# VectorE's exp groups as whole key rows, with the PV banks from the common pool

## The chip, the cores and the metric

The kernel runs on one core of one Trainium2 chip. The metric is the device time of one execution in microseconds (us). Each figure is the median of several runs; the 95% intervals come from rounds in which a kernel and the kernel before ran on the same chip.

Names: PE is TensorE, PEld its weight loads, DVE VectorE, ACT ScalarE, POOL GpSimd. A "bank" is one of the eight PSUM banks.

## The reference, cut to what matters

```python
x = A_x                                     # [1, 2048, 512], bf16
h  = x + attention(layernorm(x)) @ wo       # 32 heads of 16, softmax over 2048 keys
h2 = h + (gelu(layernorm(h) @ w_gate) * (layernorm(h) @ w_up)) @ w_down   # F = 1792
```

Attention over 32 heads of 2,048 x 2,048 scores dominates: 2,048 score tiles of 128 keys by 512 queries. The exponentials are the largest work.

## The kernel before

The kernel is a Python scheduler. It holds streams of operations with planned durations, lets the best-ranked operation that is ready go next, and so fixes one order of instructions for each engine. On the chip the engines follow these orders and wait for each other by semaphores.

A unit is one head group and query chunk: 16 key rows of four tiles. The four tiles of a row (index `g`) belong to four heads; their score matmuls use four row tiles of the PE array (32 rows each), their products with V four column tiles. ScalarE takes tiles in pairs, in order, through two pairs of banks. VectorE takes some tiles out of order, in groups of four: a conversion from PSUM (`dXE<-pbank`), two bit operations and one product (a "chain") make two fp16 factors, which cost PE two products with V per tile.

A VectorE score matmul should ride along: issued right behind a ScalarE pair, on a row tile that the pair leaves idle, it costs nearly nothing. So the scheduler plans it as `TDQ = 0.02` us. `sch.wake` holds the row tiles that the last pair used.

```python
def pick(G):                              # kernel before: the tile for a VectorE group
    ...
    cand = [i for i in range(i0, min(unit0[u + 1], i0 + AWIN))
            if i not in own and TILES[i][2] not in G["g"] | sch.wake]   # scattered over 4 rows
    return cand[0] if cand else None

def dget():
    ...
                b = yield Acquire(gate=...)           # a bank
                i = pick(G)                           # the tile is chosen here ...
                own[i] = ("d", G["k"])
                fns, rd = scores([(i, b)])
                wk = sch.wake | {TILES[i][2]}
                yield Op("pe", TDQ if TILES[i][2] not in sch.wake else TST, mode="r", ...)  # ... issued later
                sch.wake = wk
                sch.add(dconv(G, len(G["t"]), b), -2)
```

The products with V gather in a bank of their own, and a finished unit is copied out, transposed in a bank from the common pool, and scaled.

```python
PVB = 4                 # the bank for products with V
DENSE = (5, 6, 7)       # the pool for everything else
...
def ofin(u):
    yield Op("dve", 0.6, tensor_copy(OA, pbank[:, PVB, :]))
    b = yield Acquire(...)                         # a pool bank
    yield Op("pe", 4 * TTR, four transposes of OA into bank b)
    yield Op("dve", 0.165, reciprocal(...))        # reads bank b
    ... yield Op("dve", ..., tensor_tensor(Otok, ...))   # reads bank b
    sch.release(b)
...
sch.add(ofin(u), -1.0)                             # lower numbers go first
```

## Time and profile before

| kernel before | |
|---|---|
| time | 845.3 us (844.34 to 845.38) |
| span in the profile | 843.2 us |
| exps of ScalarE | 796 pairs = 1,592 tiles |
| tiles of VectorE | 456 |
| last exp ends / rest after it | 807.4 / 35.8 us |
| excess of exp intervals over 0.9035 us (those under 2 us) | 32.0 us |
| score steps / products with V of ScalarE's tiles (PE, sums of start to start) | 299 / 134 us |

How to read it: the exp records overlap, so the idle time before them understates ScalarE's lateness. The last two rows are counted from the trace's starts instead, for PE from the weight loads, of which the trace has all. The page's lines for this kernel are in the prediction below.

One more view of the kernel before, the waits: who waited for whom, us in all, times, longest.

```profile
PEld pbank L1272 <- ACT PT L1278: 221.0, 546, 1.0
PEld pbank L1272 <- DVE dXE L1590: 18.3, 50, 0.5
DVE dXE L1590 <- PE pbank L1272: 12.8, 35, 1.0
```

The first is idle time of the weight loader until ScalarE had freed a score pair's banks. It is not PE's idle time: in 215 of the 221 us matmuls issued earlier were still running, fillers among them (matmuls on zeros, `ones_bf,zero_bf`, that the scheduler puts into planned gaps of PE). So it is used only as a sign of which engine came last, not as an amount of time to be won. The other two are the exchange of pool banks for VectorE's tiles.

### The profile page before, as it was taken

Reading aid. Unit: us, or ns where it says so; the run is one execution under the profiler, and the core shown is the slowest. Engines: PE = TensorE matmul, PEld = TensorE weight load, DVE = VectorE, ACT = ScalarE, POOL = GpSimd, SP = SyncE. Lnnn points to the kernel's source line nnn. Section 1 sums busy time; section 2 is a strip of 40 time slices with the busy share of each in tenths; the row PEclk is TensorE's granted clock in tenths of the full one; section 3 lists DMA queues with packets and bytes.
Section 4 is the critical chain, followed back from the end, with each engine's and each line's share of the span. In section 5 each row is a group of like instructions: output and inputs, shape, how many; then the busy total and the mean of one; then the engine's idle time right before and its main releaser. Section 6 shows DMA issues by size and latency. Waiting matters only on the chain.

```text
span 843.2 us, 16693 instructions
## 1 busy us (share of the span) xinstructions
PE 819.5 (97%) x6773; PEld 254.4 (30%) x6773; DVE 769.0 (91%) x1246; ACT 786.3 (93%) x833; POOL 42.9 (5%) x100
## 2 busy tenths in 40 slices
PE   8999999999999999999999989999999989999997
PEld 3222222222222222222222222222233333333455
DVE  7569999999999999999989989999999999899862
ACT  3979999999999999999999999999999999999941
POOL 5600000000010000000010000000010000000000
PEclk9999999999999999999999999999999999999999
DMA  6000004300000000000000000000000000000000
GB/s 200 1 1 1 1 2 160 116 1 1 8 7 1 2 1 2 7 26 7 2 14 1 1 1 2 7 26 7 2 21 7 2 1 2 2 26 14 2 13 18
DMA packets 12327, 15.06 MB, mean 18 GB/s; under 512 B 1744, under 2 KB 11216, under 8 KB 12240
## 3 DMA queue, kind: packets, MB, share of 16 engines
q1 hardware_dynamic: 12240, 13.90, 5.0%
q8 instruction: 55, 0.90, 0.4%
q14 instruction: 32, 0.26, 0.1%
HBM read 11.80 MB, written 2.10 MB: 16 GB/s over the span
## 4 chain that ended last, share of the span: by engine, by line
PE 75%; ACT 12%; DVE 6%; issue 5%; POOL 1%; ACTq 0%; POOLq 0%; DVEq 0%
PE pbank L1272 46%; PE pbank L1271 21%; ACT PT L1278 11%; PE pbank L1870 3%; DVE dXE L1590 2%; DVE dXE L1607 1%; PE pbank L1275 1%; ACT GUT L1809 1%; PE pbank L1867 1%; PE pbank L1880 1%; DVE dXE L1605 1%; POOL xn_sb L1369 1%; DVE dW L1604 1%; PE pbank L1725 0%; PE pbank L1747 0%
## 5 line engine op out<-in xcount | busy, mean ns | idle before, releaser
L1278 ACT ACTIVATE PT<-pbank 128x1024 bf16<-128x1024 f32 x796 | 742.3, 1072 | 17.7 <-PE pbank L1272 14.6
L1272 PE MATMUL pbank<-QT,KT 32*128 32x512 bf16 x2048 | 345.0, 384 | 7.2 <-ACT PT L1278 4.9
L1590 DVE TENSOR_SCALAR dXE<-pbank 128x512 uint16<-128x512 f32 x456 | 296.9, 682 | 15.9 <-PE pbank L1272 12.8
L1272 PEld LDWEIGHTS pbank<-QT,KT 32*128 32x128 bf16 x2048 | 84.2, 91 | 311.5 <-ACT PT L1278 220.8
L1272 PE MATMUL pbank<-PT,VA 128*17 128x512 bf16 (+1 forms) x1992 | 149.4, 339 | 0.1
L1607 DVE TENSOR_TENSOR dXE<-dW,dXE 128x2048 f16<-128x2048 f16 (+1 forms) x115 | 139.1, 1210 | 2.0
L1604 DVE TENSOR_SCALAR dW<-dXE 128x2048 uint16<-128x2048 uint16 (+1 forms) x115 | 78.1, 679 | 0.8
L1605 DVE TENSOR_SCALAR dXE<-dXE 128x2048 uint16<-128x2048 uint16 (+1 forms) x115 | 78.1, 679 | 0.0
L1272 PE MATMUL pbank<-dXE,VA 128*17 128x512 f16 (+1 forms) x1136 | 70.3, 339 | 0.0
L1271 PE MATMUL pbank<-hnT_c,wu_sb 128*128 128x512 bf16 (+1 forms) x280 | 59.7, 346 | 7.4 <-DVE GUT L1823 6.8
L1271 PE MATMUL pbank<-hnT_c,wg_sb 128*128 128x512 bf16 (+1 forms) x280 | 65.5, 340 | 0.0
L1271 PE MATMUL pbank<-wd_sb,GUT 128*128 128x512 bf16 x224 | 59.2, 382 | 0.0
L1272 PEld LDWEIGHTS pbank<-PT,VA 128*17 128x17 bf16 x1992 | 39.2, 88 | 65.3 <-issue 57.8
L1870 PE MATMUL pbank<-ones_bf,zero_bf 128*128 128x512 bf16 x168 | 55.7, 386 | 0.0
L1823 DVE TENSOR_TENSOR GUT<-pbank,GUT 128x512 bf16<-128x512 f32 x56 | 37.3, 685 | 16.0 <-PE pbank L1271 12.8
L1741 POOL TENSOR_SCALAR rstd<-mv 128x1 f32<-128x1 f32 x16 | 6.6, 413 | 761.0 <-DVE mv L1739 761.0
L1271 PE MATMUL pbank<-xnT,wqkv_sb 128*128 128x512 bf16 x128 | 37.8, 383 | 0.0
L1271 PEld LDWEIGHTS pbank<-hnT_c,wu_sb 128*128 128x128 bf16 x280 | 23.5, 99 | 32.5 <-issue 11.8
L1797 DVE CAST GUT<-pbank 128x512 bf16<-128x512 f32 x49 | 33.1, 680 | 0.0
L1271 PEld LDWEIGHTS pbank<-hnT_c,wg_sb 128*128 128x128 bf16 x280 | 19.5, 97 | 27.8 <-issue 20.6
L1272 PEld LDWEIGHTS pbank<-dXE,VA 128*17 128x17 bf16 x1136 | 18.7, 88 | 29.8 <-issue 24.0
L1271 PEld LDWEIGHTS pbank<-wd_sb,GUT 128*128 128x128 bf16 x224 | 17.0, 97 | 27.0 <-issue 14.3
(82 smaller groups left out, 390.8 us busy)
## 6 DMA issues: line engine op xcount, KB each, us to landing
xres<-in_A_x_dram SPq DMA_DIRECT2D x16, 128.0 KB, 2.2
out_dram<-out_sb SPq DMA_DIRECT2D x16, 128.0 KB, 1.7
wg_sb<-in_B_w_gate_dram SPq DMA_DIRECT2D x1, 1792.0 KB, 7.1
wu_sb<-in_B_w_up_dram SPq DMA_DIRECT2D x1, 1792.0 KB, 11.2
wd_sb<-in_B_w_down_dram SPq DMA_DIRECT2D x1, 1792.0 KB, 17.4
x_sb<-in_A_x_dram SPq DMA_DIRECT2D x3, 512.0 KB, 8.3
wqkv_sb<-in_A_wqkv_dram SPq DMA_DIRECT2D x1, 896.0 KB, 7.5
x_sb<-in_A_x_dram SPq DMA_DIRECT2D x2, 256.0 KB, 2.9
```

Source lines behind the costliest of these rows:

```text
L1271: return lambda e: e.matmul(o, l, r, start=start, stop=stop)
L1272: return lambda e: e.matmul(o, l, r, start=start, stop=stop, tile_position=tile)
L1275: return lambda e: e.transpose(out=o, in_=i, identity=idn)
L1278: return lambda e: e.activation(out=o, in_=i, func=func, **kw)
L1369: lambda e: e.tensor_scalar(out=xn_sb[:, t % 8, :], in0=x_sb[:, t, :], scalar1=rstd[:, tt_], scalar2=htmp[:, tt_], op0=ALU.mult, op1=ALU.add),
L1590: yield Op("dve", 0.603, lambda e: e.tensor_scalar(out=dXE[G["k"] % NX][:, 0, j, :], in0=pbank[:, b, :], scalar1=XMIN + 1024.0 * CENTER, s ...
L1604: yield Op("dve", t1, lambda e: e.tensor_scalar(out=W.bitcast(U16), in0=X, scalar1=0x3ff, scalar2=0xb800, op0=ALU.bitwise_and, op1=ALU.bit ...
L1605: yield Op("dve", t1, lambda e: e.tensor_scalar(out=E, in0=X, scalar1=0x7c00, scalar2=0x8, op0=ALU.bitwise_and, op1=ALU.bitwise_or), reads ...
L1607: yield Op("dve", t2, lambda e: e.tensor_tensor(out=X.bitcast(F16), in0=W, in1=X.bitcast(F16), op=ALU.mult), reads=kW + kX, writes=kX, por ...
L1797: yield Op("dve", 0.6, lambda e: e.tensor_copy(out=o_ap, in_=i_ap), reads=[("pb", b)], writes=keys, extra=dE)
L1823: yield Op("dve", 0.6, lambda e: e.tensor_tensor(out=o_ap, in0=u_ap, in1=o_ap, op=ALU.mult), reads=[("pb", b)] + keys, writes=keys)
L1870: fill_op = Op("pe", TMM, lambda e: e.matmul(pbank[:, PVB, :], zero_bf[:], ones_bf[:], start=False, stop=False, skip_group_check=True), re ...
```

## The change

Its intent: a VectorE group becomes one whole key row, so that what is left for ScalarE is whole rows too, and products with V always fill four column tiles. Products with V take a bank from the pool, so that a second unit can open before the first is copied out. A second buffer for the chain and fewer gates keep more groups in flight; VectorE starts after 12 projections instead of 20. `behind()` is to pace dense work. The option to give products to GpSimd is zero. The core of the diff, cut:

```diff
-PVB = 4
-DENSE = (5, 6, 7)
+DENSE = (4, 5, 6, 7)
+DMAX = 3
+KEND = 2
+PACE = 1.0
+DB = 1
+CHP = -2.1
+NPOOL = 0
-AHEAD = 12
+AHEAD = 8
-DFROM = 20
+DFROM = 12
...
+            u, i0 = find()                       # the next free whole row
+            G = C["gopen"] = dict(u=u, t=[], row=range(i0, i0 + 4), k=C["gk"], conv=0)
+            for i in G["row"]:
+                own[i] = ("d", G["k"])
...
-                b = yield Acquire(gate=lambda: "qkdone" in C or over(G) or pick(G) is not None)
+                b = yield Acquire(gate=lambda: pick(G) is not None and C["dout"] < DMAX - (DB if behind() else 0))
                 i = pick(G)
...
-        cand = [i for i in range(i0, min(unit0[u + 1], i0 + AWIN)) if i not in own and TILES[i][2] not in G["g"] | sch.wake]
+        cand = [i for i in G["row"] if i not in G["t"] and (ANYG or TILES[i][2] not in sch.wake)]
...
-            sch.add(ofin(u), -1.0)
+            sch.add(ofin(u), -1.0).dyn = lambda: -3 if C["oa"] <= u else -1.0
...
+                    pvbank[u] = yield Acquire(prio=-20, gate=lambda: u not in pvbank and u - 1 <= C["oa"])
...
+        sch.add(group_pv(G), -5.1)               # products of a VectorE group: a stream of its own
```

## The prediction

> **What bounds the kernel now.** I read the page first, for the engines' shares and the costliest groups.
>
> ```profile
> PE 819.5 (97%) x6773; PEld 254.4 (30%) x6773; DVE 769.0 (91%) x1246; ACT 786.3 (93%) x833; POOL 42.9 (5%) x100
> L1278 ACT ACTIVATE PT<-pbank 128x1024 bf16<-128x1024 f32 x796 | 742.3, 1072 | 17.7 <-PE pbank L1272 14.6
> L1272 PE MATMUL pbank<-QT,KT 32*128 32x512 bf16 x2048 | 345.0, 384 | 7.2 <-ACT PT L1278 4.9
> L1590 DVE TENSOR_SCALAR dXE<-pbank 128x512 uint16<-128x512 f32 x456 | 296.9, 682 | 15.9 <-PE pbank L1272 12.8
> L1607 DVE TENSOR_TENSOR dXE<-dW,dXE 128x2048 f16<-128x2048 f16 (+1 forms) x115 | 139.1, 1210 | 2.0
> L1870 PE MATMUL pbank<-ones_bf,zero_bf 128*128 128x512 bf16 x168 | 55.7, 386 | 0.0
> ```
>
> There are 2,048 score tiles of 128x512. ScalarE exponentiates 1,592 of them in 796 pairs; VectorE does 456 in 115 groups. All three large engines look nearly full, and ScalarE waited only 17.7 us before its exps, so one would say that ScalarE is the bound. That reading is too quick. I therefore took the starts of the 796 exps from the trace: 454 of the 795 intervals are 0.90 us, the pace of ScalarE when nothing holds it. The excess of the longer intervals over 0.9035 us, leaving out the seven of over 2 us (four of them hold a GELU), is 32 us; the longer ones without a GELU add some 5. A record is 1.02 to 1.3 us long and overlaps the next, so a wait inside an interval hardly shows as idle time. About 9 of these 32 us lie between 40 and 100 us, some 27, with the waits of over 2 us, between 100 and 800.
>
> The timeline shows who holds them. PE matmuls and exps, first where exps keep their pace, then where they do not (start, length, engine, line; xN is the number of matmuls):
>
> ```profile
> 151.83 0.39 PE L1272 MATMUL pbank<-QT,KT 32*128 32x512 bf16 x4
> 152.16 0.61 PE L1272 MATMUL pbank<-dXE,VA 128*17 128x512 f16 x8
> 152.75 0.39 PE L1272 MATMUL pbank<-QT,KT 32*128 32x512 bf16 x3
> ...
> 153.61 0.60 PE L1272 MATMUL pbank<-QT,KT 32*128 32x512 bf16 x3
> 154.14 0.61 PE L1272 MATMUL pbank<-PT,VA 128*17 128x512 bf16 x8
> 154.69 0.39 PE L1272 MATMUL pbank<-QT,KT 32*128 32x512 bf16 x2
> ```
>
> ```profile
> 754.12 0.60 PE L1272 MATMUL pbank<-QT,KT 32*128 32x512 bf16 x3
> 754.65 0.82 PE L1271 MATMUL pbank<-wd_sb,GUT 128*128 128x512 bf16 x3
> 755.40 0.39 PE L1272 MATMUL pbank<-QT,KT 32*128 32x512 bf16 x3
> 755.73 0.82 PE L1271 MATMUL pbank<-wd_sb,GUT 128*128 128x512 bf16 x3
> 756.48 0.60 PE L1272 MATMUL pbank<-QT,KT 32*128 32x512 bf16 x3
> ```
>
> PE alternates between one score pair and one slot of other work. A score step of 0.39 takes 0.32 from its start to the next start, one of 0.60 takes 0.53; a slot takes 0.54, or 0.75 with three dense matmuls. The usual turn is 0.32 + 0.54 = 0.86 us, just under ScalarE's 0.90. A doubled score step makes it 1.07, and so do three down-projection matmuls. Two pairs of score banks let PE be one step late, no more. So **PE sets the pace in part of the turns, ScalarE in the others, and VectorE is close behind**: its busy time by windows is 671 of the 700 us from 100 to 800 and 62.8 of the 80 us from 20 to 100.
>
> ```profile
> 20.00:40.00 20.00, 18.69 (x137) 5.83 (x136) 13.15 (x31) 18.69 (x20) 15.42 (x39) 1.00 0.00 1
> 40.00:100.00 60.00, 59.89 (x410) 14.87 (x408) 49.65 (x77) 54.27 (x59) 0.00 (x0) 1.00 0.00 1
> ```
>
> In these windows (PE, PEld, DVE, ACT, POOL) PE is full of projections, VectorE is partly idle, and its first exp tile comes only at 52.7 us.
>
> **What the Trainium skill says.** "TensorEngine Tiling (Array Packing)", Key Properties: tiles of the array work independently, and a change of the tiling mode drains TensorE. The trace agrees with both: two to four score matmuls on different row tiles take 0.39 us like one, and a step costs about 0.10 us over its 0.22 of streaming. "TensorE: Matmul & The Clock Gate", Back-to-back issue gap: N/2.4 + 2.5 ns warm, 216 ns for 512 columns; here a second matmul of the same tile lengthens a step by 0.21 to 0.22 us. "VectorE: DVE Perf Modes", Why PSUM operands drop a tier: fp32 from PSUM runs at the basic rate. Agrees: 0.68 us for 512 elements from PSUM, the same as for 2,048 of 16 bits in the mask operations. "Perfetto Trace Analysis", Identifying the Most-Contended Engine: matmul busy time is no good measure. It is so here: the 97% holds 203 filler matmuls (168 on L1870, 35 on L1880).
>
> **The change part by part.**
>
> Whole rows, products of the ScalarE tiles with V. Their four tiles of a key row stand on four column tiles and run together; a slot handles two rows. Today VectorE takes scattered tiles, so a slot of 5, 6 or 7 matmuls still lasts as long as one of 8: in the trace's order of matmuls 119 such slots of the 512-wide units, and of those with 4 only about 20, take the short 0.33. All 256 slots cost at most 512 steps of 0.215 us, less about 20. With whole rows the 1,592 tiles make 398 steps. Saved: (512 - 20 - 398) x 0.215 = **20 us of PE**.
>
> Whole rows, scores. With scattered tiles the next two ScalarE tiles can lie on the same row tile and run after each other. 141 score steps in the trace cost 0.5 to 0.62 instead of 0.32. With whole rows the pairs are always (0,1) or (2,3), and a VectorE tile is taken only on an idle row tile. Saved: up to 141 x 0.215 = **30 us of PE**. Together 50 us, of some 780 us of attention.
>
> Products of VectorE tiles: 115 groups with two products per tile, 0.43 us each, unchanged. They become a stream of their own, so the unit's last products no longer wait in line for a chain.
>
> VectorE: nothing is removed. A group costs 4 x 0.60 + 2 x 0.61 + 1.14 = 4.76 us start to start (timeline). "All products stay" means that GpSimd takes none. The doubled dW and the lifted gate keep two groups in flight, and the start after 12 instead of 20 projections lets VectorE use idle time before 52 us. One group more takes two ScalarE steps away, 1.81 us.
>
> PV banks: one bank joins the three common ones. While one unit is open there are three others, as now; at a unit's end two are held, leaving two. This removes the wait for the eviction of the PV bank (0.68 us, 32 times, mostly hidden), and costs some bank pressure.
>
> Pacing: chunk 4's up and down products now run at 798 to 816 us, beside the last exps (ending at 807.4). Finished earlier, they free the way to the tail's first gate product at 819.4: **1 to 2 us**. The tail itself stays.
>
> **The sum.** Of the 36 us of late exps, about 8 come from three-matmul down steps and stay; from the early projections perhaps half of 9. I take 17 us as removed. VectorE now does 734 us between 20 and 800; in a stretch 17 us shorter, at 96.5% use, 736 fit: its share stays at about 115 groups, or 2 more at 98% (3.6 us). So 17 + 1 to 3 + 1 to 2: about 20 us, 825. Bank pressure is the one cost I can't size; for it I add 2: **827 us**.
>
> **Rivals.** First, VectorE becomes the bound: with PE free it has only 29 us idle from 100 to 800, 22.7 of it before exp operations as gaps that nobody's wait explains. If it cannot fill them, it loses groups as the span shrinks, each giving 1.8 us back to ScalarE: gain 10 to 12, time 833 to 836. Second, banks: with two PV banks held and up to three VectorE tiles outstanding, dense work lacks banks, falls behind, and the pace check cuts VectorE's tiles; then 838 to 848. For it: VectorE's largest named wait is already for scores (12.8 us). Against: a unit lasts 24 us and the overlap a few. Third, the gain is larger: stalls vanish, early VectorE idle time gives three groups, the tail 3 us: 814 to 818. Fourth, ScalarE was the bound after all and freed PE time turns to fillers: 840.
>
> **Range and chances.** The 2% line is 828.4. First and main case lie on both sides of it. 8 in 10: 815 to 841. Faster 0.53, same 0.43, slower 0.04.
>
> **What would show it.** Right: nearly no score step of 0.60; slots of V products with 4 or 8 matmuls only, the 4s short; the excess of exp intervals down from 32 to under 18 us; VectorE tiles 448 to 476; VectorE at 96% or more from 100 to 800; more PE idle or fillers; a first VectorE exp before 40 us. Wrong: VectorE tiles under 440 (first rival), or waits of dense work and of L1590 for banks at unit ends (second). Few late exps but no shorter span would mean that what PE gave was taken back in VectorE's share.

## More of the kernel before

All runs used here are with a mean granted TensorE clock of 0.988 to 1.0. Where one of the smaller differences may hang on the clock, the text says so.

A planned duration that is wrong does not make the result wrong, only the order ill-chosen.

One line of the page that the prediction does not show, the products with V of ScalarE's tiles:

```profile
L1272 PE MATMUL pbank<-PT,VA 128*17 128x512 bf16 (+1 forms) x1992 | 149.4, 339 | 0.1
```

VectorE operations that read a pool bank are lifted to rank -2.2 (`HELD`), unless their stream has a rank of its own (`dyn`).

## The result, and the profile after

The changed kernel took **864.5 us** (863.73 to 865.05), against 845.3: the ratio is 1.0232, with a 95% interval of 1.0218 to 1.0247. It is slower by over 2%. Ratios are the mean time of one kernel's fast runs over that of the other's of the same rounds, so not quite the ratio of the medians.

The page of the changed kernel, for the lines shown of before:

```profile
PE 824.8 (96%) x6713; PEld 261.6 (30%) x6822; DVE 770.2 (89%) x1229; ACT 796.3 (92%) x835; POOL 41.2 (5%) x100
L1295 ACT ACTIVATE PT<-pbank 128x1024 bf16<-128x1024 f32 x800 | 754.9, 1039 | 23.7 <-PE pbank L1289 17.1
L1289 PE MATMUL pbank<-QT,KT 32*128 32x512 bf16 x2048 | 377.4, 383 | 12.4 <-ACT PT L1295 5.9
L1601 DVE TENSOR_SCALAR dXE<-pbank 128x512 uint16<-128x512 f32 x448 | 299.1, 686 | 30.9 <-PE pbank L1289 25.5
L1619 DVE TENSOR_TENSOR dXE<-dW,dXE 128x2048 f16<-128x2048 f16 x112 | 136.7, 1220 | 2.0
L1289 PE MATMUL pbank<-PT,VA 128*17 128x512 bf16 (+1 forms) x2004 | 130.6, 339 | 0.2
L1908 PE MATMUL pbank<-ones_bf,zero_bf 128*128 128x512 bf16 x229 | 77.4, 386 | 2.8 <-issue 1.9
```

The score matmuls are as many as before, 2,048, but PE is busy with them for 377 us instead of 345. VectorE has 8 tiles fewer, and ScalarE four exp pairs more.

The waits of the changed kernel, the same three as before:

```profile
PEld pbank L1289 <- ACT PT L1295: 176.5, 438, 0.9
PEld pbank L1289 <- DVE dXE L1601: 37.7, 117, 0.7
DVE dXE L1601 <- PE pbank L1289: 25.5, 82, 1.1
```

The weight loader waited less for ScalarE (176 us against 221), so ScalarE came last less often, and the waits for banks of VectorE's tiles doubled in both directions. The change was to relieve PE and did the opposite. By the weight loads it also has 265 fillers against 203, so PE's busy time alone says little; e1_late below has 289 and is 19 us faster, so their number is not the loss.

The account of the 18.9 us by which the span grew: the excess of exp intervals under 2 us rose from 32.0 to 49.0 (17.0 us); four exps more, at 0.9035 us, are 3.6; the intervals of over 2 us without a GELU cost 2.1 less. The first exp starts 0.6 earlier. The rest after the last exp grew from 35.8 to 42.7 us, but 6.1 of it is only moved: the fourth GELU stood between two exps before (an interval of 6.99 us) and now follows the last. That leaves 0.8. The sum is 18.7.

**Where the score time comes from.** PE and ACT of the changed kernel (start, length, engine, line; xN matmuls):

```profile
158.69 0.39 PE L1289 MATMUL pbank<-PT,VA 128*17 128x512 bf16 x4
159.02 0.60 PE L1289 MATMUL pbank<-QT,KT 32*128 32x512 bf16 x3
159.55 0.61 PE L1908 MATMUL pbank<-ones_bf,zero_bf 128*128 128x512 bf16 x2
160.09 0.60 PE L1289 MATMUL pbank<-QT,KT 32*128 32x512 bf16 x3
...
162.02 1.02 ACT L1295 ACTIVATE PT<-pbank 128x1024 bf16<-128x1024 f32 x1 [0.19 <-PE pbank L1289]
```

The product slot with four matmuls is short (0.39), as intended. But a pair with one VectorE tile takes 0.60 us, twice in a row: two of its three matmuls are on the same row tile and run after each other. A little later an exp waits 0.19 us for its scores. In the order of instructions one can count this: give each matmul one step on its row tile, in order, and count the steps beyond those of the pairs. The kernel before has 149 extra steps, the changed kernel **237**; at 0.215 us these are 32 and 51 us. By the weight loads, score steps took 330 us of PE in place of 299, while products of ScalarE's tiles with V fell from 134 to 115.

Why more? The tile is chosen when the bank is granted, but issued when VectorE has drained that bank, and by then other PE work has often come between. With scattered tiles such a late matmul met the next pair on one of its row tiles in 85 of 133 cases. With whole rows pairs alternate between row tiles (0,1) and (2,3): a tile chosen to suit the pair (0,1) lies on 2 or 3, which is just what the next pair uses. It now clashed in 157 of 177. Whole rows alone do not make it so certain: in e5_before_rows below, counted in nearly the same way, it is 106 of 155. How long after the choice the matmul is issued counts as well.

**Where the banks went.** After the four transposes of a finished unit come the reciprocal and the scaling, which free the bank. First a unit of the kernel before, then one of the changed kernel:

```profile
788.10 0.40 PE L1275 MATMUL pbank<-ident,OA 128*128 128x128 bf16 x4
788.59 0.25 DVE L1681 RECIPROCAL LINV<-pbank 128x16 f32<-128x16 bf16 x1
789.67 0.48 DVE L1687 TENSOR_TENSOR Otok<-pbank,LINV 128x128 bf16<-128x128 bf16 x2
```

```profile
83.67 0.40 PE L1292 MATMUL pbank<-ident,OA 128*128 128x128 bf16 x4
98.57 0.25 DVE L1715 RECIPROCAL LINV<-pbank 128x16 f32<-128x16 bf16 x1
98.86 0.42 DVE L1721 TENSOR_TENSOR Otok<-pbank,LINV 128x256 bf16<-128x256 bf16 x1
```

The bank waits 15 us for a reciprocal of 0.25. Over the 32 units the mean from the transposes to the end of the scaling is 14.9 us (76.7 at most, since later units overtake earlier ones), against 1.9 before. The cause is one line of the diff: `.dyn = lambda: -3 if C["oa"] <= u else -1.0`. A stream with `dyn` is not lifted to -2.2, and once the unit is copied out its rank is -1.0, behind every other VectorE stream. A unit lasts some 24 us, so the bank gained for the pool was held by this idle tail for over half of the time.

### The profile page after: what moved, and what is told of

It reads as the page before. It is cut to its first block, busy times and chain, and to the rows that moved or that the text cites. A ratio compares the mean times of both kernels' runs of the same rounds, so it can differ in the third digit from the quotient of the medians.

```text
span 862.1 us, 16680 instructions
## 1 busy us (share of the span) xinstructions
PE 824.8 (96%) x6713; PEld 261.6 (30%) x6822; DVE 770.2 (89%) x1229; ACT 796.3 (92%) x835; POOL 41.2 (5%) x100
## 4 chain that ended last, share of the span: by engine, by line
PE 77%; DVE 10%; ACT 5%; issue 3%; POOL 1%; ACTq 0%; DVEq 0%; POOLq 0%
PE pbank L1289 48%; PE pbank L1288 21%; PE pbank L1908 5%; ACT PT L1295 4%; DVE dXE L1601 3%; DVE dXE L1619 3%; DVE dW L1615 1%; DVE dXE L1616 1%; PE pbank L1292 1%; ACT GUT L1844 1%; PE pbank L1781 1%; DVE QT L1433 0%; PE pbank L1759 0%; DVE GUT L1831 0%; DVE OA L1706 0%
## 5 line engine op out<-in xcount | busy, mean ns | idle before, releaser
L1295 ACT ACTIVATE PT<-pbank 128x1024 bf16<-128x1024 f32 x800 | 754.9, 1039 | 23.7 <-PE pbank L1289 17.1
L1289 PE MATMUL pbank<-QT,KT 32*128 32x512 bf16 x2048 | 377.4, 383 | 12.4 <-ACT PT L1295 5.9
L1289 PEld LDWEIGHTS pbank<-QT,KT 32*128 32x128 bf16 x2048 | 91.6, 91 | 317.3 <-ACT PT L1295 176.2
L1619 DVE TENSOR_TENSOR dXE<-dW,dXE 128x2048 f16<-128x2048 f16 x112 | 136.7, 1220 | 2.0
L1289 PE MATMUL pbank<-PT,VA 128*17 128x512 bf16 (+1 forms) x2004 | 130.6, 339 | 0.2
L1908 PE MATMUL pbank<-ones_bf,zero_bf 128*128 128x512 bf16 x229 | 77.4, 386 | 2.8 <-issue 1.9
L1615 DVE TENSOR_SCALAR dW<-dXE 128x2048 uint16<-128x2048 uint16 x112 | 76.9, 686 | 0.9
L1616 DVE TENSOR_SCALAR dXE<-dXE 128x2048 uint16<-128x2048 uint16 x112 | 76.7, 685 | 0.0
L1288 PE MATMUL pbank<-hnT_c,wg_sb 128*128 128x512 bf16 (+1 forms) x261 | 60.5, 336 | 2.7 <-issue 2.5
L1908 PEld LDWEIGHTS pbank<-ones_bf,zero_bf 128*128 128x128 bf16 x264 | 19.2, 96 | 49.8 <-issue 48.0
L1288 PEld LDWEIGHTS pbank<-hnT_c,wu_sb 128*128 128x128 bf16 x280 | 23.4, 98 | 23.0 <-issue 10.4
```

The lines of the kernel that those rows point to most:

```text
L1288: return lambda e: e.matmul(o, l, r, start=start, stop=stop)
L1289: return lambda e: e.matmul(o, l, r, start=start, stop=stop, tile_position=tile)
L1295: return lambda e: e.activation(out=o, in_=i, func=func, **kw)
L1615: yield Op("dve", t1, lambda e: e.tensor_scalar(out=W.bitcast(U16), in0=X, scalar1=0x3ff, scalar2=0xb800, op0=ALU.bitwise_and, op1=ALU.bit ...
L1616: yield Op("dve", t1, lambda e: e.tensor_scalar(out=E, in0=X, scalar1=0x7c00, scalar2=0x8, op0=ALU.bitwise_and, op1=ALU.bitwise_or), reads ...
L1619: yield Op("dve", t2, lambda e: e.tensor_tensor(out=X[:, 0:nd, :].bitcast(F16), in0=W[:, 0:nd, :], in1=X[:, 0:nd, :].bitcast(F16), op=ALU. ...
```

## The experiments

All twelve kernels of the table (beside before and after) gave correct results. "Extra" is the count of extra score steps in the order of instructions.

| run | what it is | DVE tiles | extra | us | ratio to before |
|---|---|---|---|---|---|
| before | | 456 | 149 | 845.3 | |
| after | the change | 448 | 237 | 864.5 | 1.0232 |
| e1_late | after + tile chosen at issue | 436 | 0 | 845.4 | 1.0005 |
| e2_ofin | after + old rank of the scaling | 464 | 215 | 854.1 | 1.0109 |
| e3_both | both edits | 456 | 0 | 835.5 | 0.9892 |
| e12_hold, e13_hold28 | e3 + bank held 7.5 us more | 432, 436 | 0 | 846.3, 842.8 | 1.0023, 0.9979 |
| e5_before_rows | before + whole rows alone | 456 | 179 | 853.2 | 1.0085 |
| e6_rows_late | e5 + issue rule | 424 | 0 | 845.3 | 1.0007 |
| e4_before_late | before + issue rule | 422 | 6 | 848.1 | 1.0040 |
| e7_honest | after, true cost planned | 468 | 189 | 865.1 | 1.0265 |
| e9_dfrom20 | e3, start after 20 projections | 448 | 0 | 840.0 | 0.9951 |
| e10_pool1 | e3 + one product on GpSimd | 460 | 0 | 832.4 | 0.9851 |
| e11_tuned | e10, two constants moved | 472 | 0 | 830.4 | 0.9821 |

Some expectations speak of the chip's lag behind the schedule: the start of each score pair on the chip, less its planned start, from the first pair to the last. It grew by 9.5 us in the kernel before and by 30.4 in the changed one.

**Tile chosen at issue (e1_late).** The matmul is issued only while `sch.wake` is fresh, and the tile is picked then:

```diff
-                i = pick(G)
-                yield Op("pe", TDQ if TILES[i][2] not in sch.wake else TST, mode="r", cols=128, fns=fns, ...)
+                op = Op("pe", TDQ, None, mode="r", cols=128, ..., gate=lambda: pick(G) is not None)
+                def bind():                          # called when the operation is issued
+                    i = cell["i"] = pick(G)
+                    op.fns = scores([(i, b)])[0]
+                op.extra = bind
+                yield op
```

> The changed kernel, but the tile of a VectorE score matmul is chosen only when it is issued: directly behind a pair of ScalarE's, on a row tile that the pair leaves idle. In the order of instructions no score step is then doubled (counted: 237 extra steps of 0.215 us in the changed kernel, 149 in the kernel before, 0 here), at the price of 436 instead of 448 VectorE tiles, so 806 exps instead of 800. Theory 'doubled score steps' (PE time that the kernel's own scheduler does not know of, since it plans every such matmul as 0.02 us): the lag of the chip behind the schedule falls from 30 us to about 10, the excess of the exp intervals over 0.9035 us from 49 to about 25, time 846 to 852. Rival 'banks' (the score steps are hidden anyway, only missing PSUM banks and the tail count): 6 exps more and nothing gained, 866 to 872.

Measured: 845.4 us, 19 us less than the changed kernel, though VectorE has 12 tiles fewer. The excess of exp intervals fell to 26.3 us, the lag to 4.3. The weight loader waits for ScalarE more than in either kernel:

```profile
PEld pbank L1289 <- ACT PT L1295: 277.3, 685, 1.3
```

The rival (866 or more) falls. In this run the bank of the next section is held for less time too (9.2 us in the mean, not 14.9), but e2_ofin and e3_both below, where it is held 2.3 and 1.6 us, differ by the same edit and by 18.7 us. The extra score steps are the larger cause.

**Old rank of the scaling (e2_ofin).**

```diff
-            sch.add(ofin(u), -1.0).dyn = lambda: -3 if C["oa"] <= u else -1.0
+            sch.add(ofin(u), -1.0)
```

> The changed kernel with one rank undone: the reciprocal and the scaling of a finished unit's output go back to the high rank that they had before (in the changed kernel they come after all other VectorE work, and the bank with the transposed output is held 14.9 us instead of 1.9 us in the trace). Theory 'banks': hold falls to under 4 us, dense work gets its bank back, VectorE gets 464 tiles instead of 448 and 792 exps, the tail after the last exp shortens from 43 to about 40 us; time 852 to 857. Theory 'doubled score steps only': 215 extra steps instead of 237 and 8 exps fewer, so at most 12 us, but the tail stays at 43 us: 855 to 862. Rival 'rows as such': no change, 864.

Measured: 854.1 us; the mean hold fell from 14.9 to 2.3 us, VectorE got 16 tiles more. The excess of exp intervals stayed at 48.4 us, so the first cause is nearly untouched (215 extra steps), as it should be.

**Both (e3_both).**

> Both edits together: no doubled score step, output scaling at its old rank; 456 VectorE tiles and 796 exps, as in the kernel before. If the two causes account for the loss: 838 to 845, so no slower than the kernel before, and the excess of exp intervals under 25 us. If something else in the change costs (a PV bank from the common pool, whole rows as such): 850 or more.

Measured: 835.5 us, 1.1% faster than the kernel before, under the 2% that would count as faster. The time is below the expected range, while the excess, 25.1 us, just misses "under 25"; the hold is 1.6 us. Together the two edits undo 29 us, so they account for the loss and more. The steps of this version (PE, then the wait):

```profile
158.16 0.61 PE L1915 MATMUL pbank<-ones_bf,zero_bf 128*128 128x512 bf16 x2
158.75 0.39 PE L1289 MATMUL pbank<-QT,KT 32*128 32x512 bf16 x2
...
161.50 0.40 PE L1289 MATMUL pbank<-QT,KT 32*128 32x512 bf16 x4
161.83 0.61 PE L1915 MATMUL pbank<-ones_bf,zero_bf 128*128 128x512 bf16 x2
162.42 0.39 PE L1289 MATMUL pbank<-QT,KT 32*128 32x512 bf16 x3
```

```profile
PEld pbank L1289 <- ACT PT L1295: 283.7, 689, 1.1
```

Steps of two, three and four score matmuls all last 0.39 to 0.40 us. (L1915 are fillers; this version has 254, the changed kernel 265.)

**Is it the held bank or the order of VectorE's work (e12_hold, e13_hold28)?** A wait after the transposes holds the bank while the rank stays high; the second leaves the last four units alone:

```diff
         C["ofd"] = u + 1
+        if u < NU - 4:                            # only in e13_hold28
+            t0 = sch.now
+            yield Wait(lambda: sch.now >= t0 + 7.5)
```

> The version with both edits (835.5 us), with one thing put back: the bank with a finished unit's transposed output is held for 7.5 us more before its reciprocal is planned, while the rank of that work stays high. The schedule then gives VectorE 432 tiles instead of 456 (808 exps instead of 796). Theory 'the held bank is what the low rank costs': 843 to 848, near the 845.4 us of the version with the low rank (hold 9.2 us there). Rival 'the order of VectorE's work costs, not the bank': it stays at 834 to 838.

> The same as the run with the held bank, but the last four units are not held, so that the added wait cannot lie in the tail: what is left is the bank's absence during attention. The schedule gives VectorE 436 tiles and 806 exps, as many as the version with the low rank. Theory 'the held bank is what the low rank costs': 840 to 846, so at least half of the 10 us between the low rank (845.4) and the old one (835.5). Rival 'the held bank cost only through the tail's wait': 834 to 838.

Measured: 846.3 and 842.8 us. In the first the rest after the last exp is 41.5 us against 35.9, partly because the fourth GELU fell behind the exps and perhaps because of the last unit's own wait; that is why the second was run. It shows 7.3 of the 9.9 us that separate e1_late from e3_both. So the absence of the bank is most of what the low rank costs; the remaining 2.6 us are open.

**Whole rows alone, and the rule without the rest (e5_before_rows, e6_rows_late, e4_before_late).** In the kernel before, only the choice of tiles was replaced by the row version (`pick`, with a whole row reserved when a group opens); then the matmul was gated to be issued directly behind a pair on an idle row tile; then that gate alone with scattered tiles:

```diff
-        cand = [i for i in range(i0, ...) if i not in own and TILES[i][2] not in G["g"] | sch.wake]
+        cand = [i for i in G["row"] if i not in G["t"] and TILES[i][2] not in sch.wake]   # e5, e6
-                yield Op("pe", TDQ if ... else TST, mode="r", ...)
+                yield Op("pe", TDQ, mode="r", ..., gate=lambda: sch.wake and TILES[i][2] not in sch.wake)   # e6, e4
```

> The kernel before with whole key rows for VectorE's groups alone: dedicated PV bank, old gates, old ranks; 456 VectorE tiles, 796 exps, 179 extra score steps against 149 before (6.5 us more), while the products with V should save 16 us of PE. Theory 'doubled score steps' : the saving is about eaten, 842 to 854. My prediction's view (whole rows relieve PE by 50 us): 830 to 836. Rival 'rows as such cost the 19 us': 860 or more.

> The kernel before with whole rows (853.2 us) and the rule that a VectorE score matmul is issued only directly behind a pair on an idle row tile; dedicated PV bank, old gates and ranks. No doubled score step, but only 424 VectorE tiles, 812 exps. Theory 'doubled score steps cost about their length': 845 to 851, 16 exps more (14 us) against some 38 us of PE and the stalls by it. The difference to the 835.5 us of the version with both edits is then what the other parts of the change (PV banks from the pool, a second group in flight, the early start) are worth: 10 us or more. Rival 'the other parts are worth nothing': 836 or less.

> The kernel before, scattered tiles as they are, with only the rule that a VectorE score matmul is issued directly behind a pair on an idle row tile (its tile is fixed beforehand, and waits for such a place). No doubled step but for 6 repeated pairs, but only 422 VectorE tiles and 813 exps against 456 and 796. Theory 'what a doubled step costs, a lost VectorE tile costs as well': 848 to 854, no gain over the kernel before. If the rule were a gain of its own: 840 or less.

Measured: 853.2, 845.3 and 848.1 us. Whole rows by themselves make the kernel slower, by 8 us in the median; three of the four runs had a mean clock of 0.993, and the one at 1.0 took 849.7 us, so about 5 us of it remain at full clock. With the same 456 tiles, products with V take 114 us of PE instead of 134, score steps 309 instead of 299, and there are more late exps (excess 34.4 us and two more long waits than before). The rule takes these away, but where it has to wait for its place VectorE loses 32 to 34 tiles, so that neither version passes the kernel before. The rows pay only with more of the change: from 845.3 (e6) to 835.5 (e3). These 9.8 us, just under the expected 10, are not the other parts alone: e3_both also chooses its tile at issue, which e6 does not, and e6 ran at a clock of 0.989 to 0.994 against 0.999.

**A scheduler that knows the cost (e7_honest).**

```diff
         end = start + op.dur                     # the core of the edit; where op.row is set is cut
+        if op.mode == "r" and (not self.wake or op.row in self.wake):
+            end = start + TST
```

> The changed kernel, whose scheduler charges a VectorE score matmul 0.213 us instead of 0.02 where it is not issued on an idle row tile behind a pair; the choice of tiles is as in the changed kernel. The order still has 189 extra score steps (237 in the changed kernel). If the loss is the PE time of these steps: 853 to 865, little better than 864.5. If the loss was that the schedule did not know of them, and so placed other work badly: 845 or less. The lag of the chip behind the schedule should fall from 30 us to under 8 either way.

Measured: 865.1 us, no better, with a lag of 3.1 us. So knowing the cost is not enough, and the lag as such is not the loss. That the PE time itself is the loss, this run does not show: it has 48 extra steps fewer than the changed kernel, and gains some 20 us by it and by 10 exps fewer (the excess is 38.2 us, not 49.0). It loses them again elsewhere: the intervals of over 2 us without a GELU cost 14 us more (in two of them the exp waited for PE while 32 and 24 products with V ran in a row), and the rest after the last exp is 49.7 us, not 42.7. Why this schedule orders its work so is open. That the steps had to be avoided rests on e1 and e3.

**The early start (e9_dfrom20).**

```diff
-DFROM = 12
+DFROM = 20
```

> The version with both edits, but VectorE's tiles start after 20 projections as before, not 12. The schedule gives 448 tiles instead of 456, and 800 exps. My prediction took the early start for 1 to 3 us: 836 to 839. Rival 'the early start only takes PE time from the projections': 835 or less.

Measured: 840.0 us, so the early start is worth 4.5 us here, a little more than expected; against the two runs at a clock of 0.998, as in e3_both (839.2 and 839.3 us), it is 3.8.

**One product on GpSimd, and two constants (e10_pool1, e11_tuned).**

```diff
-NPOOL = 0
+NPOOL = 1
-AHEAD = 8
+AHEAD = 9      # e11_tuned only
-HLAG = 8
+HLAG = 7       # e11_tuned only
```

> The version with both edits, with one of a group's four products on GpSimd (the option that the change leaves at zero). The schedule takes 1.11 us for it and gives VectorE 460 tiles and 794 exps. If GpSimd's product runs beside VectorE's work as planned: 830 to 833. Rival 'both engines hold each other up': 836 or more, with longer VectorE operations in the trace than the 0.68 and 1.22 us of now.

> The version with both edits and one product on GpSimd (832.4 us), with two constants moved: rows are taken 9 tiles ahead instead of 8, and freed PE time is given to dense work at a lag of 7 instead of 8. The schedule gives an end 7 us earlier than that version's. As the chip follows the schedule within 5 us where no step is doubled: 824 to 828, faster than the kernel before by over 2%.

Measured: 832.4 and 830.4 us. VectorE's chain in e3_both, then in e10_pool1 with GpSimd's product:

```profile
L1626 DVE TENSOR_TENSOR dXE<-dW,dXE 128x2048 f16<-128x2048 f16 x114 | 139.2, 1221 | 2.5
L1623 DVE TENSOR_SCALAR dXE<-dXE 128x2048 uint16<-128x2048 uint16 x114 | 77.9, 683 | 0.0
```

```profile
L1628 POOL TENSOR_TENSOR dXE<-dW,dXE 128x512 f16<-128x512 f16 x115 | 147.5, 1283 | 540.4 <-DVE dXE L1626 540.4
L1626 DVE TENSOR_TENSOR dXE<-dW,dXE 128x1536 f16<-128x1536 f16 x115 | 109.6, 953 | 2.1
L1623 DVE TENSOR_SCALAR dXE<-dXE 128x2048 uint16<-128x2048 uint16 x115 | 83.2, 723 | 0.0
```

The two engines do get in each other's way (683 ns became 723, and GpSimd took 1,283 ns against 1,110 planned), but the 0.27 us saved per group is more. The means hide how: 109 of the 115 operations on L1623 took 0.68 to 0.69 us as in e3_both, and six took 1.04 to 1.65; GpSimd's product took about 1.15 us 76 times and 1.53 us 39 times. So keeping all products on VectorE is not the better choice in the mended version. e11_tuned missed its 824 to 828 in the median: its lag grew to 10.2 us, and the page shows the granted clock dip to 0.7 in one slice. Half of the lag came there: by the windows the clock was 0.92 from 600 to 620 us and 0.73 from 620 to 640, and the lag rose from 3.5 us at 600 to 8.5 at 640. The four runs go the same way: 831.5 and 831.3 us at a mean clock of 0.989, 829.4 at 0.995, 827.9 at 0.997, the clock of the kernel before; that last one lies inside the forecast. Why the clock dipped, no run here separates. It is the fastest version, 1.8% under the kernel before.

**Without a run.** Setting `DB` to zero in the changed kernel gives the same program byte for byte: the pacing never acts there. A dedicated PV bank with the rest of the change could not be tried: the streams then wait for each other and the schedule stretches to 988 us. So what the pooled PV bank alone is worth stays open.

## Why the prediction was wrong

Measured 864.5 us, outside 815 to 841; a gain was forecast, a loss came. By its steps:

- **What bounds the kernel**: right. PE sets the pace in part of the turns, and the excess of exp intervals is the measure of it; every run without doubled steps, or with only six (e4), brought it down to between 20 and 29 us, and e7_honest, with 189 left, to 38. One reading was wrong: not 9 of the 32 us lie between 40 and 100 us, but 2.7, or 7.4 with the two intervals of over 2 us there; the half that the sum took from it was too much.
- **Whole rows, products with V**: right. "Saved: (512 - 20 - 398) x 0.215 = 20 us of PE"; the weight loads show 134 to 115.
- **Whole rows, scores**: this step failed. It said that "a VectorE tile is taken only on an idle row tile. Saved: up to 141 x 0.215 = 30 us of PE". It read the condition in `pick` as if it held when the matmul is issued. It holds when the bank is granted. Score steps rose by 31 us. The doubled ScalarE pairs, which I blamed for the 141 long steps, were only 8 in the kernel before: nearly all were VectorE matmuls issued late. The sign turned because late matmuls clashed more often (157 of 177 in place of 85 of 133), and because more of them were late. Whole rows alone bring 30 of the 88 additional extra steps (e5: 179); the other 58 come with the rest of the change, and which part of it makes them was not separated.
- **PV banks**: "costs some bank pressure", sized at 2 us, with the doubt placed in two PV banks held at a unit's end. The pressure was real, but its cause is another line of the same diff, which I had not read for its rank: the scaling behind all other VectorE work. Giving it its old rank is worth 10.4 us (after to e2) or 9.9 (e1 to e3).
- **VectorE**: 448 tiles, at the lower edge of "448 to 476". The early start, taken for 1 to 3 us, measured 4.5 in the mended version (3.8 at like clocks). Two signs of being right failed: VectorE was busy for 656 of the 700 us from 100 to 800 (94%, not 96), and its first exp came at 42.5 us, not before 40.
- **Pacing**: no gain; it does nothing in this build, and the last GELU moved behind the last exp.
- **The rivals**: the second, banks, named the right direction and a right symptom (waits of L1590's successor for scores and banks doubled), but at 838 to 848 it was too small without the score steps.

Part of what I hoped for is there: without extra steps and with the bank freed, whole rows and the rest give 835.5 us, about 4 of the 10 us by the early start. What the rows alone give of the others is not separated. Against the 827 of the prediction that is still 8 us short: the excess is 25 us, not under 18.

## What to carry to other kernels

A condition that a scheduler tests when it reserves a resource says nothing about the moment of issue; where the cost hangs on what stands next to an instruction, choose at issue, and count neighbours in the final order rather than in the code that made it. A regular pattern is only as good as its phase: alternating pairs make a tile that fits now clash one step later. And look for the scratch bank whose last reader has the lowest rank: here a reciprocal of 0.25 us held an eighth of PSUM for 15 us.

## What the Trainium skill lacked or had wrong

- "Perfetto Trace Analysis", Identifying the Most-Contended Engine, calls occupancy a fair measure for the Scalar engine. Here it hid the problem: ACT was busy for 692 of the 700 us from 100 to 800 in the kernel before, that is 8 us idle, yet the exp intervals there exceeded their pace by 27 us, since records of 1.02 to 1.3 us overlap at a pace of 0.90. The intervals between starts showed it.
- "TensorEngine Tiling (Array Packing)", Key Properties, says that tiles operate independently, and gives no cost there for two matmuls on one tile inside a packed step; the prediction took it from the issue gap that it cites, rightly. Measured: 0.39 us became 0.60, and the order of the changed kernel has 237 such extra steps.
- "GPSIMD Engine Reference", Specifications, says that its SBUF interfaces are shared with VectorE and that they contend; that row gives no size. Measured in e10_pool1: the mean of VectorE's two bit operations went from 683 to 699 and 723 ns, because 3 and 6 of the 115 took 1.0 to 1.65 us while the others kept their time; GpSimd's product took 1,283 ns in the mean; and the trade still gained 3 us.
